# Three small edits to a transformer-block kernel: one query group moved ahead of a stage, three denominator sums put in one place, the last output block split in 384 and 128 columns

## The chip, the cores and the metric

The kernel runs on one core of one Trainium2 chip. The metric is the device time of one execution in microseconds (us). Beside it each run has a span, from the first to the last instruction in the trace of the core.

In the lines of the profile PE is TensorE (matmuls), PEld is TensorE's weight load (the stationary operand of a matmul), DVE is VectorE, ACT is ScalarE, POOL is GpSimd and SP is SyncE; a "q" behind it means the engine's sequencer, and "issue" is time in which an engine waited for nothing that the profile shows. L98 is the line of the helper `mm`, so the stages are told apart by the tiles. The "chain" is the sequence of work that ended last, followed back from the last instruction. To evacuate a PSUM tile is to read the result of its matmuls with another engine, which frees it. The landing of a DMA is the time from its issue to the moment its data is known to have arrived, and the closing waits are SyncE's waits for all DMAs at the end of the program.

## The reference, cut to what matters

One sequence of 2048 tokens, model width 1024, 32 attention heads of 32 columns, feed-forward width 3584, all in bf16. `sa, ca, ga, sb, cb, gb` are rows of 1024 computed from a conditioning vector.

```python
h = layernorm(x) * (1 + ca) + sa
q, k, v = split(h @ wqkv)                       # 32 heads
pq, pk = phi(q), phi(k)                         # phi(t) = (t + 1 if t > 0 else exp(t)) + 1e-6
kv  = einsum('bhsd,bhse->bhde', pk, v)          # linear attention: no softmax
z   = einsum('bhsd->bhd', pk)
num = einsum('bhqd,bhde->bhqe', pq, kv)
den = einsum('bhqd,bhd->bhq', pq, z) + 1e-6     # the denominator
x = x + ga * ((num / den) @ wo)
h = layernorm(x) * (1 + cb) + sb
x = x + gb * ((silu(h @ w_gate) * (h @ w_up)) @ w_down)
```

## The kernel before: the parts that matter

The sequence is cut into four chunks of 512 tokens (`sc`, 0 to 3). `pqs[sc]` holds phi(q), transposed: eight groups (`hg`) of 128 columns by 512 tokens. `SCW`, `NB` = 512; `STC` = 4 tiles of 128 tokens in a chunk; `FC` = 28 groups of the feed-forward width; `ST` = 16 tiles in all. The code below is cut and condensed.

The denominators of a chunk are sums on TensorE. Each matmul has 32 stationary columns and writes 32 rows of one PSUM tile, so four of them can run in the array together: in the trace of before the four start 3 to 4 ns apart, and each four take 0.056 us. The reciprocals travel through DRAM to be spread over the rows of their head (`rbc`), and `den_apply` multiplies them into `pq` in four VectorE operations of two head groups each.

```python
def den_norm(sc):
    pq = pqs[sc]
    den = acc_b("den")
    for hg in range(HG):
        for q in range(STC):
            mm(den[32*q:32*q+32, 0:P], lhsT=Zden[:, hg, :], rhs=pq[:, hg, q*P:(q+1)*P], ...)
    dsum = small.tile([P, P], F32, name="dsum", bufs=2)
    nc.vector.tensor_scalar_add(out=dsum[:], in0=den[:, 0:P], scalar1=DEN_EPS)
    rb = small.tile([P, P], BF16, name="rb", bufs=2)
    nc.vector.reciprocal(out=rb[:], in_=dsum[:])
    # ... rb to DRAM and back as rbc, by POOL's DMA queue (cut) ...

def den_apply(sc):
    pq, rbc = pqs[sc], rbcs.pop(sc)
    for k in range(4):
        ks = slice(2*k, 2*k+2)
        nc.vector.tensor_tensor(out=pq[:, ks, :], in0=pq[:, ks, :], in1=rbc[:, ks, :], op=ALU.mult)
```

A query group (`q_phase`) is eight 512-column matmuls followed by phi on ScalarE and VectorE. `wo_tile` multiplies 128 tokens of `pq` by `wo` in two blocks of eight matmuls. The order of work around the first wo stage and in the first gate and up stage is this:

```python
q_phase(2, 3, 4)
with tc.issue_after(last_phi[0].ins):
    den_apply(0)
q_phase(2, 4, 5)                  # one query group between the multiplies and wo
for st in range(STC):
    wo_tile(st)
q_phase(2, 5, 8)
q_phase(3, 0, 5)
# ... modulate, q_phase(3, 5, 8) (cut) ...
def late_den(apply, norm):
    if apply: den_apply(apply)
    if norm:  den_norm(norm)

# gate_up calls an entry after its block fb of 512 feed-forward columns
gate_up(0, {0: lambda: den_norm(1), 2: lambda: late_den(1, 2), 4: lambda: late_den(2, 3),
            6: lambda: den_apply(3)})
```

The last stage is `down`. Each output block of 128 tokens by 512 columns is 28 matmuls, two VectorE operations and one DMA out:

```python
for nb in range(NNB):
    ns = slice(nb*NB, (nb+1)*NB)
    x1r = x1p.tile([P, NB], F32, name="x1r", bufs=2)
    nc.sync.dma_start(out=x1r[:], in_=x1_dram[st*P:(st+1)*P, ns])
    y_ps = acc_a()
    for f in range(FC):
        mm(y_ps[:], lhsT=guT[sc][f//GPT][:, f%GPT, t*P:(t+1)*P], rhs=wd[f//WDF][:, f%WDF, ns], ...)
    yt = ep.tile([P, NB], F32, name="e")
    nc.vector.tensor_tensor(out=yt[:], in0=y_ps[:], in1=gb_bc[:, ns], op=ALU.mult)
    ob = yp.tile([P, NB], BF16, name="ob")
    nc.vector.tensor_tensor(out=ob[:], in0=yt[:], in1=x1r[:], op=ALU.add)
    nc.sync.dma_start(out=out2[st*P:(st+1)*P, ns], in_=ob[:])
```

Of the kernel before, what the change touches and what calls it, by code (L numbers as in the profile page):

```python
# [9 lines left out]
ALU = mybir.AluOpType  # L10
BF16 = mybir.dt.bfloat16
F32 = mybir.dt.float32
# [9 lines left out]
def kernel(  # L22
# [13 lines left out]
    nc = tc.nc  # L36
    P = nc.NUM_PARTITIONS
# [4 lines left out]
    ST = S // P  # L42
# [4 lines left out]
    NSC = S // SCW  # L47
    STC = SCW // P
    NB = 512
    NNB = D // NB  # L50
# [4 lines left out]
    GPT = 8  # L55
# [4 lines left out]
    out2 = out[0]  # L60
# [12 lines left out]
    x1p = ctx.enter_context(tc.tile_pool(name="x1p", bufs=3))  # L73
    ep = ctx.enter_context(tc.tile_pool(name="ep", bufs=3))
    yp = ctx.enter_context(tc.tile_pool(name="yp", bufs=2))
    small = ctx.enter_context(tc.tile_pool(name="small", bufs=4))
# [20 lines left out]
    def mm(out, lhsT, rhs, start, stop):  # L97
        return tc.keep_in_program_order(nc.tensor.matmul(out, lhsT=lhsT, rhs=rhs, start=start, stop=stop))  # L98
# [4 lines left out]
    def big(name, shape):  # L103
        return k8.tile([P] + shape, BF16, name=name, tag="k8")

    def acc_a():
        return pa.tile([P, NB], F32, name="acc", tag="pa")

    def acc_b(name, shape=(NB,), dt=F32):
        return pb.tile([P] + list(shape), dt, name=name, tag="pb")  # L110

    x1_dram = dram.tile([S, D], F32, name="x1_scratch")
# [16 lines left out]
    for b in range(2):  # L129
        ts = []  # L130
        for q in (1, 0):
            t = big("wme", [DC, NB])
# [36 lines left out]
    gb_bc = const.tile([P, D], BF16, name="gb_bc")  # L169
# [91 lines left out]
    def phi_to(dst, acc):  # L261
        e = ep.tile([P, NB], BF16, name="eb")
        nc.scalar.activation(out=e[:], in_=acc, func=ACT.Exp)  # L263
        nc.vector.tensor_scalar(out=e[:], in0=e[:], scalar1=1.0, scalar2=PHI_EPS, op0=ALU.min, op1=ALU.add)  # L264
        last_phi.append(None)
        last_phi[0] = last_phi[-1] = nc.vector.scalar_tensor_tensor(out=dst, in0=acc, scalar=0.0, in1=e[:], op0=ALU.max, op1=ALU.add)
# [36 lines left out]
    def q_phase(sc, lo=0, hi=DC):  # L303
        if lo == 0:
            pqs[sc] = big("pq", [HG, SCW])
        for qc in range(lo, hi):
            acc = acc_a()
            for cc in range(DC):
                mm(acc[:], lhsT=wq[cc // 4][:, cc % 4, qc * P:(qc + 1) * P], rhs=hTs[sc][:, cc, :],
                                 start=(cc == 0), stop=(cc == DC - 1))  # L310
            phi_to(pqs[sc][:, qc, :], acc[:])
# [55 lines left out]

    rbcs = {}

    def den_norm(sc):  # L370
        pq = pqs[sc]
        den = acc_b("den")
        for hg in range(HG):
            for q in range(STC):
                mm(den[32 * q:32 * q + 32, 0:P], lhsT=Zden[:, hg, :], rhs=pq[:, hg, q * P:(q + 1) * P],
                                 start=(hg == 0), stop=(hg == HG - 1))
        dsum = small.tile([P, P], F32, name="dsum", bufs=2)
        nc.vector.tensor_scalar_add(out=dsum[:], in0=den[:, 0:P], scalar1=DEN_EPS)
        rb = small.tile([P, P], BF16, name="rb", bufs=2)
        with nc.allow_low_precision("bf16 reciprocal multiplies bf16 phi(q)"):  # L380
            nc.vector.reciprocal(out=rb[:], in_=dsum[:])
        for q in range(STC):
            nc.gpsimd.dma_start(out=rden_dram[sc, :, q * P:(q + 1) * P], in_=rb[32 * q:32 * q + 32, :])
        rbc = big("rbc", [HG, SCW])
        rv = rden_dram[sc].rearrange("(h g) t -> h (g t)", h=HPC)
        for h in range(HPC):
            nc.gpsimd.dma_start(out=rbc[h * DH:(h + 1) * DH].rearrange("p g t -> p (g t)"),
                                in_=rv[h].unsqueeze(0).to_broadcast([DH, HG * SCW]))
        rbcs[sc] = rbc
# [4 lines that stand above are left out]
            ks = slice(2 * k, 2 * k + 2)  # L394
            nc.vector.tensor_tensor(out=pq[:, ks, :], in0=pq[:, ks, :], in1=rbc[:, ks, :], op=ALU.mult)  # L395
# [89 lines left out]
    for h in range(2):  # L485
        hs = slice(4 * h, 4 * h + 4)
        nc.vector.tensor_tensor(out=KVZ[:, hs, :], in0=kv_acc[:, hs, 0:P],
                                in1=kvmask[:].unsqueeze(1).to_broadcast([P, 4, P]), op=ALU.mult)
        nc.vector.tensor_tensor(out=Zden[:, hs, :], in0=kv_acc[:, hs, P:P + 1].to_broadcast([P, 4, DH]),
                                in1=zmask[:, hs, :], op=ALU.mult)  # L490
# [3 lines left out]
        transpose(tpk[:, hg, :], KVZ[:, hg, :])  # L494
    nc.scalar.copy(out=KVT[:, 0:4, :], in_=tpk[:, 0:4, :])
    nc.vector.tensor_copy(out=KVT[:, 4:8, :], in_=tpk[:, 4:8, :])
    den_norm(0)
    q_phase(1, 4, 5)
    wf = [(hg, nb) for hg in range(HG) for nb in range(NNB)]
    for qc in range(5, 11):  # L500
# [40 lines left out]
    guT = {}  # L541
# [3 lines left out]
    def gate_up(sc, between=None):  # L545
        guT[sc] = []
        for fb in range(NFB):
            wb = []
            for view in (wg_v, wu_v):
                w = big("wgu", [DC, FBW])  # L550
                last_w[sc] = nc.sync.dma_start(out=w[:], in_=view[:, :, fb * FBW:(fb + 1) * FBW])
                wb.append(w)
            for fj in range(FPB):
                f = fb * FPB + fj
                if f % GPT == 0:
                    guT[sc].append(big("gu", [min(GPT, FC - f), SCW]))
                ps = []
                for w in wb:
                    acc = acc_a()
                    for cc in range(DC):  # L560
                        last_mm[sc] = mm(acc[:], lhsT=w[:, cc, fj * P:(fj + 1) * P], rhs=h2Ts[sc][:, cc, :],
                                              start=(cc == 0), stop=(cc == DC - 1))
                    ps.append(acc)
                sg = ep.tile([P, NB], F32, name="e")
                nc.scalar.activation(out=sg[:], in_=ps[0][:], func=ACT.Silu)  # L565
                gm = nc.vector.tensor_tensor(out=guT[sc][f // GPT][:, f % GPT, :], in0=ps[1][:], in1=sg[:], op=ALU.mult)  # L566
            if between and fb in between:
                with tc.issue_after(gm.ins):
                    between[fb]()

    def down(sc, side):
        for t in range(STC):
            st = sc * STC + t
            for nb in range(NNB):
                ns = slice(nb * NB, (nb + 1) * NB)
                x1r = x1p.tile([P, NB], F32, name="x1r", bufs=2)
                nc.sync.dma_start(out=x1r[:], in_=x1_dram[st * P:(st + 1) * P, ns])
                y_ps = acc_a()
                for f in range(FC):
                    mm(y_ps[:], lhsT=guT[sc][f // GPT][:, f % GPT, t * P:(t + 1) * P],  # L580
                                     rhs=wd[f // WDF][:, f % WDF, ns], start=(f == 0), stop=(f == FC - 1))
                yt = ep.tile([P, NB], F32, name="e")
                nc.vector.tensor_tensor(out=yt[:], in0=y_ps[:], in1=gb_bc[:, ns], op=ALU.mult)  # L583
                ob = yp.tile([P, NB], BF16, name="ob")
                nc.vector.tensor_tensor(out=ob[:], in0=yt[:], in1=x1r[:], op=ALU.add)  # L585
                nc.sync.dma_start(out=out2[st * P:(st + 1) * P, ns], in_=ob[:])
                if side:
                    with tc.issue_after(last_mm[sc].ins):
                        side.pop(0)()

    q_phase(2, 3, 4)
    with tc.issue_after(last_phi[0].ins):
        den_apply(0)
    q_phase(2, 4, 5)
    for st in range(STC):
        wo_tile(st)
    q_phase(2, 5, 8)
    q_phase(3, 0, 5)
    with tc.issue_after(last_phi[0].ins):
        modulate_all(h2Ts[0], cb1T, sbT)  # L600
    q_phase(3, 5, 8)

    def late_den(apply, norm):
        if apply:
            den_apply(apply)
        if norm:
            den_norm(norm)

    gate_up(0, {0: lambda: den_norm(1), 2: lambda: late_den(1, 2), 4: lambda: late_den(2, 3),
                6: lambda: den_apply(3)})  # L610
    wd = []
    for b in range(FC // WDF):
        w = big("wd", [WDF, D])
# [2 lines left out]
    for sc in range(NSC):  # L616
        if sc > 0:
            gate_up(sc)
        side = []
        if sc + 1 < NSC:  # L620
            side = [lambda st=(sc + 1) * STC + t: wo_tile(st) for t in range(STC)]
        down(sc, side)
# [29 lines left out]
```

## Time and profile before

| | before |
|---|---|
| time, median of the runs beside the first run of the change | 847.84 us (847.76 to 847.96) |
| span of the profiled execution | 846.2 us |
| TensorE busy | 838.6 us, 99% |
| granted TensorE clock | 0.999 |

At 99% busy there seems to be nothing left to gain. But "busy" does not say that the engine moves at its best rate, and on a span of 846 us the missing 1% is 8 us. So one looks where the stream of matmuls is broken. In the stages without an interruption, 588 matmuls of 512 columns take 126.91 us in the chain, that is 0.2158 us each. Everything above that rate is loss.

**The first wo stage.** From the chain of waits of before (start us, length us, what):

```profile
180.57 1.74 PE acc L98 x8
...
182.96 0.31 DVE eb L264
...
183.29 0.04 DVE pq L266
...
183.90 0.69 DVE pq L395
184.59 0.05 issue
184.64 14.50 PE a_ps L98 x64
```

The chain leaves TensorE at 182.31 (the end of query group 3), goes over VectorE, and comes back at 184.64. The 64 wo matmuls then take 14.50 us where 64 x 0.2158 are 13.81. The timeline of the weight loads of before shows why (start, length, engine, line, operation; in brackets the idle time before it and what ended it):

```profile
183.43 0.10 PEld L98 LDWEIGHTS <-wq 128*128 128x128 bf16 x1
184.64 0.11 PEld L98 LDWEIGHTS <-pq 128*128 128x128 bf16 x2 [1.11 <-DVE pq L395]
185.24 0.11 PEld L98 LDWEIGHTS <-pq 128*128 128x128 bf16 x2 [0.49 <-DVE pq L395]
185.84 0.11 PEld L98 LDWEIGHTS <-pq 128*128 128x128 bf16 x2 [0.49 <-DVE pq L395]
186.44 0.55 PEld L98 LDWEIGHTS <-pq 128*128 128x128 bf16 x4 [0.49 <-DVE pq L395]
```

Two head groups are loaded, then TensorE waits for the next multiply of `den_apply(0)`, three times over. VectorE finishes one multiply every 0.60 us, and TensorE uses up two head groups in 0.43.

**The denominator sums.** From the timeline of TensorE in before, the first of the three blocks:

```profile
228.76 3.19 PE L98 MATMUL acc<-h2T,wgu 128*128 128x512 bf16 x14
231.87 0.63 PE L98 MATMUL den<-pq,Zden 128*32 128x128 bf16 x32
232.44 1.90 PE L98 MATMUL acc<-h2T,wgu 128*128 128x512 bf16 x8
```

The single records behind these lines: the last gate matmul starts at 231.565, the den matmuls at 231.874, and the next gate matmul at 232.437. Of those 0.872 us, 0.216 are the first matmul's own slot. So a block costs 0.656 us, and its eight head groups, 0.056 us apart, are only 0.45 of it.

The same trace has controls for reading the other 0.21 as the price of the 32-column mode. Where the matmuls go from 512 to 129 columns of `rhs`, with 128 stationary columns throughout (acc to kvp, at 64.999) and back (66.814), the next matmul starts one ordinary slot later, 0.216 and 0.056 us. Where 32 stationary columns begin or end, it does not: from acc to den it is 0.309 (0.093 more than the slot), from kvp to modr, the other matmuls with 32 stationary columns, 0.149 (0.093 more), and from modr back to acc 0.311 (0.095 more).

**The tail.** From the chain of before:

```profile
672.52 169.23 PE acc L98 x784
841.74 0.02 issue
841.77 0.70 DVE e L583
842.47 0.02 issue
842.49 0.69 DVE ob L585
```

After the last matmul come two VectorE operations on 512 columns, then the output DMA (issued at 843.214), its landing, and the closing waits, until 846.19. That is 4.46 us without any TensorE work.

### The profile page before, as it was taken

To read this page: it belongs to the slowest core of one execution; us is meant where nothing else is said; L and a number is where in the kernel's file an instruction comes from. 1 tells how busy PE (TensorE), PEld (TensorE's weight loads), DVE (VectorE), ACT (ScalarE), POOL (GpSimd) and SP (SyncE) were. 2 spreads that over 40 slices of the span, in tenths; PEclk is the share of its full clock that TensorE was granted. 3 is DMA by queue.
4 is the path that set the end of the run, shared out by engine and by line. 5 is a ranking of instruction groups with operands and counts; after the bars stand their busy time and mean duration, and the time that the engine had idled before them with its cause. 6 is when DMAs were issued, how large, how long until landed. Compare 5 with 4: busy or idle time off the path is not lost.

```text
span 846.2 us, 10498 instructions
## 1 busy us (share of the span) xinstructions
PE 838.6 (99%) x4284; PEld 385.7 (46%) x4284; DVE 307.2 (36%) x602; ACT 173.8 (21%) x267; POOL 55.7 (7%) x160
## 2 busy tenths in 40 slices
PE   8999999999999999999999999999999999999997
PEld 4445445544444444444444444444444444444443
DVE  5756464467423325431111344211114431111121
ACT  1455453354311110101111010011110101111000
POOL 2101010012011001100000010000001100000000
PEclk9999999999999999999999999999999999999999
DMA  9893870029976765528434073581604639710011
GB/s 309 301 257 98 243 187 1 1 52 215 348 210 207 214 186 174 181 69 266 146 104 149 19 236 95 159 283 54 199 1 126 185 69 318 240 59 0 19 57 50
DMA packets 125840, 128.74 MB, mean 152 GB/s; under 512 B 33376, under 2 KB 107360, under 8 KB 125280
## 3 DMA queue, kind: packets, MB, share of 16 engines
q1 hardware_dynamic: 122208, 115.36, 46.0%
q0 software_dynamic: 3584, 12.72, 5.0%
q8 instruction: 33, 0.54, 0.3%
q14 instruction: 15, 0.12, 0.0%
HBM read 108.01 MB, written 12.71 MB: 143 GB/s over the span
## 4 chain that ended last, share of the span: by engine, by line
PE 98%; DVE 1%; POOL 0%; DMA 0%; issue 0%; ACT 0%; SPq 0%; DVEq 0%; POOLq 0%
PE acc L98 88%; PE a_ps L98 7%; PE kvp L98 1%; PE modr L98 0%; PE wf L98 0%; DMA x_sb<-in_A_x_dram 0%; DVE stats L199 0%; PE mod_ps L98 0%; PE den L98 0%; POOL zmask L186 0%; PE tp L101 0%; POOL rstd L193 0%; PE bcr L98 0%; DVE e L583 0%; DVE ob L585 0%
## 5 line engine op out<-in xcount | busy, mean ns | idle before, releaser
L98 PE MATMUL acc<-h2T,wgu 128*128 128x512 bf16 x1792 | 387.9, 379 | 0.0
L98 PEld LDWEIGHTS <-wgu 128*128 128x128 bf16 x1792 | 175.1, 98 | 211.0
L98 PE MATMUL acc<-wd,gu 128*128 128x512 bf16 x896 | 196.0, 379 | 0.0
L566 DVE TENSOR_TENSOR gu<-acc,e 128x512 bf16<-128x512 f32 x112 | 77.4, 691 | 300.4 <-PE acc L98 300.4
L565 ACT ACTIVATE e<-acc 128x512 f32<-128x512 f32 x112 | 66.9, 597 | 375.2 <-PE acc L98 375.2
L98 PEld LDWEIGHTS <-gu 128*128 128x128 bf16 x896 | 87.6, 98 | 105.8
L98 PEld LDWEIGHTS <-hT 128*128 128x128 bf16 x512 | 49.6, 98 | 60.8 <-DVE hT L212 1.0
L583 DVE TENSOR_TENSOR e<-acc,gb_bc 128x512 f32<-128x512 f32 x32 | 22.1, 691 | 130.5 <-PE acc L98 130.5
L98 PE MATMUL a_ps<-wo,pq 128*128 128x512 bf16 x256 | 57.9, 379 | 0.6 <-DVE pq L395 0.6
L98 PE MATMUL acc<-hT,wq 128*128 128x512 bf16 x256 | 57.1, 379 | 0.0
L98 PE MATMUL acc<-wk,hT 128*128 128x512 bf16 x256 | 56.9, 379 | 0.0
L98 PE MATMUL acc<-wv,hT 128*128 128x512 bf16 x256 | 55.9, 379 | 0.0
L263 ACT ACTIVATE eb<-acc 128x512 bf16<-128x512 f32 x64 | 37.9, 596 | 62.8 <-PE acc L98 60.5
L209 ACT ACTIVATE xn<-x,nmr,rstd 128x1024 bf16<-128x1024 f32 x16 | 19.8, 1240 | 127.6 <-POOL nmr L207 127.6
L264 DVE TENSOR_SCALAR eb<-eb 128x512 bf16<-128x512 bf16 x64 | 18.4, 291 | 60.6 <-ACT eb L263 60.6
L98 PEld LDWEIGHTS <-pq 128*128 128x128 bf16 x256 | 24.7, 98 | 31.8 <-DVE pq L395 2.6
L98 PEld LDWEIGHTS <-wq 128*128 128x128 bf16 x256 | 24.9, 98 | 29.8
L534 POOL DMA_DIRECT2D x_scratch<-x x16 | 9.6, 600 | 369.6 <-DVE x L527 369.6
L527 DVE TENSOR_TENSOR x<-a_ps,x_sb 128x512 f32<-128x512 f32 x32 | 22.1, 691 | 8.0 <-PE a_ps L98 7.9
L193 POOL TENSOR_TENSOR rstd<-veps,neg_half 128x1 f32<-128x1 f32 x32 | 18.2, 569 | 81.3 <-DVE veps L191 70.4
L301 ACT CAST v<-acc 128x512 bf16<-128x512 f32 x32 | 18.3, 582 | 22.1 <-PE acc L98 22.1
L528 DVE BATCH_NORM_STATS2 stats<-x 128x6 f32<-128x512 f32 x32 | 22.2, 695 | 1.1
(72 smaller groups left out, 280.7 us busy)
## 6 DMA issues: line engine op xcount, KB each, us to landing
wgu<-in_B_w_gate_dram SPq DMA_DIRECT2D x28, 1024.0 KB, 7.4
wgu<-in_B_w_up_dram SPq DMA_DIRECT2D x28, 1024.0 KB, 8.7
x_sb<-in_A_x_dram SPq DMA_DIRECT2D x32, 256.0 KB, 5.9
wml<-in_w_mod_dram SPq DMA_DIRECT2D x8, 1024.0 KB, 8.6
x_scratch<-x POOLq DMA_DIRECT2D x16, 512.0 KB, 3.1
x1r<-x_scratch SPq DMA_DIRECT2D x32, 256.0 KB, 3.0
wd<-in_B_w_down_dram SPq DMA_DIRECT2D x7, 1024.0 KB, 7.7
wme<-in_w_mod_dram SPq DMA_DIRECT2D x4, 1024.0 KB, 11.2
```

The costliest lines, as they stand in the source:

```text
L98: return tc.keep_in_program_order(nc.tensor.matmul(out, lhsT=lhsT, rhs=rhs, start=start, stop=stop))
L193: nc.gpsimd.tensor_tensor(out=rstd[:, 0:n], in0=veps[:, 0:n], in1=neg_half[:].to_broadcast([P, n]), op=ALU.pow)
L209: nc.scalar.activation(out=dst, in_=src, func=ACT.Identity, bias=nmr[:], scale=rstd[:, 0:1])
L263: nc.scalar.activation(out=e[:], in_=acc, func=ACT.Exp)
L264: nc.vector.tensor_scalar(out=e[:], in0=e[:], scalar1=1.0, scalar2=PHI_EPS, op0=ALU.min, op1=ALU.add)
L301: nc.scalar.copy(out=v[:, t, nb * 4:(nb + 1) * 4, 0:P], in_=acc[:].rearrange("p (g e) -> p g e", e=P))
L527: nc.vector.tensor_tensor(out=x1[:, ns], in0=a_ps[:], in1=x_t[:, ns], op=ALU.add)
L528: nc.vector.bn_stats(out=stats[:, nb, :], in_=x1[:, ns])
L534: nc.gpsimd.dma_start(out=x1_dram[st * P:(st + 1) * P, :], in_=x1[:])
L565: nc.scalar.activation(out=sg[:], in_=ps[0][:], func=ACT.Silu)
L566: gm = nc.vector.tensor_tensor(out=guT[sc][f // GPT][:, f % GPT, :], in0=ps[1][:], in1=sg[:], op=ALU.mult)
L583: nc.vector.tensor_tensor(out=yt[:], in0=y_ps[:], in1=gb_bc[:, ns], op=ALU.mult)
```

## The change

Each edit aims at one of the three places. The diff, cut to its core:

```diff
-    def den_norm(sc):
+    def den_sum(sc):                     # matmuls, sum, reciprocal
...
+    def den_spread(sc):                  # rb to DRAM and back as rbc
...
+            pieces = [(0, NB), (NB, NB)] if st < ST - 1 else [(0, NB), (NB, 384), (NB + 384, 128)]
+            for lo, width in pieces:     # in down(): load, 28 matmuls, two VectorE operations, DMA out
...
     q_phase(2, 3, 4)
     with tc.issue_after(last_phi[0].ins):
         den_apply(0)
-    q_phase(2, 4, 5)
+    q_phase(2, 4, 6)
     for st in range(STC):
         wo_tile(st)
-    q_phase(2, 5, 8)
+    q_phase(2, 6, 8)
...
-    gate_up(0, {0: lambda: den_norm(1), 2: lambda: late_den(1, 2), 4: lambda: late_den(2, 3),
-                6: lambda: den_apply(3)})
+    def late_den(sc, sums=()):
+        for s in sums:
+            den_sum(s)
+        if sc > 1:
+            den_apply(sc - 1)
+        if sc < NSC:
+            den_spread(sc)
+
+    gate_up(0, {0: lambda: late_den(1, range(1, NSC)), 2: lambda: late_den(2), 4: lambda: late_den(3),
+                6: lambda: late_den(NSC)})
```

`den_norm(0)` becomes `den_sum(0)` and `den_spread(0)`; `dsum` goes to one buffer and `rb` to four.

More of the change, by code (lines that the diff above doesn't have):

```diff
@@ L368 @@
     rbcs = {}
-    def den_norm(sc):
+    rbs = {}
+    def den_sum(sc):
         pq = pqs[sc]
@@ L376, in den_norm @@
                                  start=(hg == 0), stop=(hg == HG - 1))
-        dsum = small.tile([P, P], F32, name="dsum", bufs=2)
+        dsum = small.tile([P, P], F32, name="dsum", bufs=1)
         nc.vector.tensor_scalar_add(out=dsum[:], in0=den[:, 0:P], scalar1=DEN_EPS)
-        rb = small.tile([P, P], BF16, name="rb", bufs=2)
+        rb = rbs[sc] = small.tile([P, P], BF16, name="rb", bufs=4)
         with nc.allow_low_precision("bf16 reciprocal multiplies bf16 phi(q)"):
             nc.vector.reciprocal(out=rb[:], in_=dsum[:])
+    def den_spread(sc):
+        rb = rbs.pop(sc)
         for q in range(STC):
@@ L496 @@
     nc.vector.tensor_copy(out=KVT[:, 4:8, :], in_=tpk[:, 4:8, :])
-    den_norm(0)
+    den_sum(0)
+    den_spread(0)
     q_phase(1, 4, 5)
@@ L573, in down @@
             st = sc * STC + t
-            for nb in range(NNB):
-                ns = slice(nb * NB, (nb + 1) * NB)
-                x1r = x1p.tile([P, NB], F32, name="x1r", bufs=2)
-                nc.sync.dma_start(out=x1r[:], in_=x1_dram[st * P:(st + 1) * P, ns])
-                y_ps = acc_a()
+            pieces = [(0, NB), (NB, NB)] if st < ST - 1 else [(0, NB), (NB, 384), (NB + 384, 128)]
+            for lo, width in pieces:
+                ns = slice(lo, lo + width)
+                x1r_t = x1p.tile([P, NB], F32, name="x1r", bufs=2)
+                x1r = x1r_t[:, 0:width]
+                nc.sync.dma_start(out=x1r, in_=x1_dram[st * P:(st + 1) * P, ns])
+                y_acc = acc_a()
+                y_ps = y_acc[:, 0:width]
                 for f in range(FC):
-                    mm(y_ps[:], lhsT=guT[sc][f // GPT][:, f % GPT, t * P:(t + 1) * P],
+                    mm(y_ps, lhsT=guT[sc][f // GPT][:, f % GPT, t * P:(t + 1) * P],
                                      rhs=wd[f // WDF][:, f % WDF, ns], start=(f == 0), stop=(f == FC - 1))
-                yt = ep.tile([P, NB], F32, name="e")
-                nc.vector.tensor_tensor(out=yt[:], in0=y_ps[:], in1=gb_bc[:, ns], op=ALU.mult)
-                ob = yp.tile([P, NB], BF16, name="ob")
-                nc.vector.tensor_tensor(out=ob[:], in0=yt[:], in1=x1r[:], op=ALU.add)
-                nc.sync.dma_start(out=out2[st * P:(st + 1) * P, ns], in_=ob[:])
+                yt_t = ep.tile([P, NB], F32, name="e")
+                yt = yt_t[:, 0:width]
+                nc.vector.tensor_tensor(out=yt, in0=y_ps, in1=gb_bc[:, ns], op=ALU.mult)
+                ob_t = yp.tile([P, NB], BF16, name="ob")
+                ob = ob_t[:, 0:width]
+                nc.vector.tensor_tensor(out=ob, in0=yt, in1=x1r, op=ALU.add)
+                nc.sync.dma_start(out=out2[st * P:(st + 1) * P, ns], in_=ob)
                 if side:
@@ L601 @@
     q_phase(3, 5, 8)
-    def late_den(apply, norm):
-        if apply:
-            den_apply(apply)
-        if norm:
-            den_norm(norm)
-    gate_up(0, {0: lambda: den_norm(1), 2: lambda: late_den(1, 2), 4: lambda: late_den(2, 3),
-                6: lambda: den_apply(3)})
+    def late_den(sc, sums=()):
[7 more added lines that the diff above has]
+                6: lambda: late_den(NSC)})
     wd = []
```

## The prediction

> **What bounds the kernel now.** The page gives TensorE 838.6 of 846.2 us busy (99%) at a granted clock of 0.999. The chain of waits that ended last is 98% PE. From about 16 us on, TensorE streams 512-column matmuls every 0.2158 us (126.91 us for 588 in the chain) and is broken in three places only, and each edit of the change is aimed at one.
>
> 1. *The first wo stage.* The timeline has the last query group (2, 4) at 182.1 to 183.9 us; the next weight load would be due at about 183.67. The first four loads of pq come at 184.64, 185.24, 185.84 and 186.44 instead: each waits for a 0.69 us multiply of den_apply(0), one every 0.60 us, while two matmuls use only 0.43. The load for head group 6 is due at 184.95 and comes at 186.44, so 1.49 us are lost. The 64 wo matmuls agree: 14.50 us instead of 13.81, after a late start of about 0.8.
> 2. *Denominator sums.* From the last 512-column matmul before a den block to the first after it are 0.872 us; 0.216 is that matmul's own slot, so a block costs 0.66. Its body is eight head groups at 0.056 us, or 0.45 (four 32-column tiles overlap). The other 0.21 are entering and leaving the 32-column mode. The Trainium skill ("TensorEngine Tiling (Array Packing)", Key Properties) says that changing the tiling mode drains TensorE; the gap on each side of the block here, about 0.1 us, agrees.
> 3. *The tail.* Matmuls end at 841.74; two VectorE operations on 128x512 (0.69 each) take until 843.21; the issue, landing (1.7 us) and final semaphore waits take until 846.2.
>
> **What the change does.**
> 1. One more query group (1.73 us) stands between den_apply(0) and wo. The built order keeps the four multiplies ahead of the phi operations of groups 4 and 5, so the multiplies still end at 184.6, 185.2, 185.8 and 186.4; loads are then due at 185.4, 185.8, 186.3 and 186.7. The wait goes, with 0.3 us to spare. Gain 1.47 us. The evacuation of wo starts about 1.3 us later on VectorE (188.5), but there are four PSUM tiles. h2T and the first gate weights come about 1 us later while gate_up starts 1.5 us sooner; their slack (about 3 us or more) should hold.
> 2. Three blocks become one: two exits and entries fewer, 2 x 0.21 = 0.41 us gained. VectorE gets 3 x 1.26 us of sums and reciprocals at once, under the 5 us until the gate/up evacuation needs it. No stall.
> 3. 28 extra matmuls. By the 129-column kvp matmuls (0.056 us apart), the last block grows by about 0.08 us. The last two VectorE operations shrink from 0.69 to about 0.29 us (dsum, 128 columns, takes 0.28): 0.80 gained. The 384 columns are evacuated during the last 28 matmuls. DMA latency is mostly fixed: the skill ("DMA: Bandwidth & Descriptors", two cost components) says about 2 us; 1.7 here, so nothing to gain. The last DMA's semaphore moves two places on in the closing waits (0.06 us each): 0.12. Net 0.84.
>
> Sum 2.7 us, all on the critical path: **845.1 us**, 8 in 10 within 844.7 to 845.8. Faster by over 2%: 0.00; within 2%: 1.00; slower: 0.00.
>
> **What would show it.** No VectorE wait before the first pq load; wo's 64 matmuls in 13.8 us; one den piece of about 1.45 us in the chain; last two VectorE operations near 0.29 us.
>
> **What would make it wrong.** Late h2T or wgu at the first gate matmul; VectorE's later wo evacuation filling the PSUM tiles; 128-column matmuls limited by weight loads (+0.7 us if 0.08 each); a slower landing of 256-byte rows.

## The result, and the profile after

The median is 845.63 us (four runs: 845.4, 845.63, 845.63, 847.27) against 847.84 us before. The ratio is 0.9974, with a 95% interval of 0.996 to 0.9989: a gain clear of the noise. The profiled span is 843.5 us against 846.2. The output was correct.

The first wo stage, from the chain of after: TensorE does not leave it any more, and the 64 matmuls take 13.81 us.

```profile
180.70 5.18 PE acc L98 x24
185.88 13.81 PE a_ps L98 x64
199.69 31.08 PE acc L98 x144
230.77 1.45 PE den L98 x96
232.22 89.03 PE acc L98 x412
```

The fourth line is the one den block that took the place of three. From the timeline of TensorE in after:

```profile
230.70 1.52 PE L98 MATMUL den<-pq,Zden 128*32 128x128 bf16 x96
```

The weight loads of after (timeline) have no wait in brackets:

```profile
183.34 2.04 PEld L98 LDWEIGHTS <-wq 128*128 128x128 bf16 x10
185.50 3.12 PEld L98 LDWEIGHTS <-pq 128*128 128x128 bf16 x15
```

The tail, from the chain of after. The two operations now take 0.30 and 0.29 us:

```profile
670.90 169.30 PE acc L98 x812
840.20 0.02 issue
840.23 0.30 DVE e L593
840.53 0.02 issue
840.55 0.29 DVE ob L596
```

And this is the timeline of VectorE in after, near the end: the 384 columns are evacuated while TensorE works on the last 128, and VectorE is then idle for 0.41 us before the last piece.

```profile
838.66 0.56 DVE L593 TENSOR_TENSOR e<-acc,gb_bc 128x384 f32<-128x384 f32 x1 [3.13 <-PE acc L98]
839.25 0.56 DVE L596 TENSOR_TENSOR ob<-e,x1r 128x384 bf16<-128x384 f32 x1
840.23 0.29 DVE L593 TENSOR_TENSOR e<-acc,gb_bc 128x128 f32<-128x128 f32 x1 [0.41 <-PE acc L98]
840.55 0.29 DVE L596 TENSOR_TENSOR ob<-e,x1r 128x128 bf16<-128x128 f32 x1
```

The landing of the last output DMA, in before and then in after (finer figures are given with the tail experiments):

```profile
DMA to landing us min/median/max: 1.7/1.7/1.7
DMA to landing us min/median/max: 1.5/1.5/1.5
```

All three mechanisms are visible as predicted. Two things are not as predicted. The span fell by 2.7 us and the time by only 2.2. And the time from the last output DMA's issue to the end fell by 0.35 us (2.98 to 2.63), where 0.12 had been forecast.

### The profile page after: what moved, and what is told of

It reads as the page before. It is cut to its first block, busy times and chain, and to the rows that moved or that the text cites. A ratio compares the mean times of both kernels' runs of the same rounds, so it can differ in the third digit from the quotient of the medians.

```text
span 843.5 us, 10565 instructions
## 1 busy us (share of the span) xinstructions
PE 838.6 (99%) x4312; PEld 388.2 (46%) x4312; DVE 307.8 (36%) x604; ACT 173.8 (21%) x267; POOL 55.7 (7%) x160
## 4 chain that ended last, share of the span: by engine, by line
PE 99%; DVE 0%; ACT 0%; issue 0%
PE acc L98 90%; PE a_ps L98 7%; PE kvp L98 1%; PE modr L98 0%; PE wf L98 0%; PE mod_ps L98 0%; PE tp L101 0%; PE den L98 0%; PE bcr L98 0%; ACT hT L220 0%; DVE hT L221 0%; PE mcol L98 0%; DVE e L593 0%; DVE ob L596 0%; DVE sel L402 0%
## 5 line engine op out<-in xcount | busy, mean ns | idle before, releaser
L98 PE MATMUL acc<-wd,gu 128*128 128x512 bf16 (+2 forms) x924 | 196.1, 373 | 0.0
L98 PEld LDWEIGHTS <-gu 128*128 128x128 bf16 x924 | 89.3, 98 | 104.5
L593 DVE TENSOR_TENSOR e<-acc,gb_bc 128x512 f32<-128x512 f32 (+2 forms) x33 | 22.3, 676 | 130.1 <-PE acc L98 130.1
L596 DVE TENSOR_TENSOR ob<-e,x1r 128x512 bf16<-128x512 f32 (+2 forms) x33 | 22.3, 675 | 1.0
```

The source lines that it names most:

```text
L98: return tc.keep_in_program_order(nc.tensor.matmul(out, lhsT=lhsT, rhs=rhs, start=start, stop=stop))
L593: nc.vector.tensor_tensor(out=yt, in0=y_ps, in1=gb_bc[:, ns], op=ALU.mult)
L596: nc.vector.tensor_tensor(out=ob, in0=yt, in1=x1r, op=ALU.add)
```

## The experiments

Twelve runs were made, on two chips (m_mid, t_onedma, t256 and t448 on one, the rest on the other). Each was timed against the kernel before in the same rounds. The first expectations speak of 1.6 us between time and span in before, and of 0.5 us of growth. That was 847.84, a median of four runs, less the one profiled span of 846.2; the later calls, with time and span of each run, have 1.84 to 1.89 in the median, and 0.3 us of growth. First the three parts alone, and the change once more.

### One part at a time

**g_only**: the kernel before with `q_phase(2, 4, 6)` and `q_phase(2, 6, 8)`, nothing else.

> The kernel before with one more query group ahead of the first wo stage, nothing else. Theory (three separate stalls that add up): the span falls by 1.3 us, the loss counted from the matmul starts of the two traces (the prediction had 1.47, counted from the weight loads); the 64 wo matmuls take 13.8 us without a wait for the multiplies. Rival (the stall only moves on): the later evacuation on VectorE comes back as a wait before the first gate matmul, and the span falls by under 0.6 us. On the 0.5 us by which time minus span grew from before to after: if it belongs to the last block, it does not show here and the time falls by about 1.3 too; if it differs from program to program or from load to load, it may show here.

Measured: 846.73 us against 848.09 (median of five and nine runs), span 844.85, which is 1.34 us less than before, ratio 0.9986 (0.9973 to 0.9998). No weight load waits for the multiplies, and the chain stays on TensorE from the query groups through wo. The rival, a stall that only moves on, falls. Time minus span is 1.89 us, and before it was also 1.89 in the same rounds.

**d_only**: the kernel before with `den_sum` and `den_spread` and the new hooks of the first gate and up stage.

> The kernel before with the sums of chunks 1 to 3 in one place, nothing else. Theory: the span falls by 0.42 us (two times the 0.21 of entering and leaving the 32-column mode); the den block is one piece of about 1.45 us. Rival (the saved 0.4 us of after is something else, a wait that moved): the span falls by under 0.15 us, or VectorE's six operations in a row make TensorE wait for an accumulator. Time minus span: as before (1.6 us) if the last block is its cause.

Measured: 847.56 us, span 845.73, 0.46 less than before. By the starts of the matmuls around it, the block of 96 costs 1.549 us, and the three of before cost 0.656, 0.657 and 0.657: a gain of 0.42. VectorE's six operations in a row delay nothing. The ratio of times is 0.9992 (0.9979 to 1.0004): by the times alone this gain does not stand clear of the noise, and it rests on the trace.

**t_only**: the kernel before with the last block in 384 and 128 columns.

> The kernel before with the last block in 384 and 128 columns, nothing else. Theory: the span falls by 1.1 us (0.80 by the two short VectorE operations, 0.23 by a faster landing, 0.12 by the place of the semaphore among the closing waits, less 0.07 for the extra matmuls). Rival for the last two: the landing differs from run to run, and the span falls by 0.8 us alone. Time minus span: if the 0.5 us belongs to the last block, the time falls by only 0.6 us and time minus span is 2.1 us, as in after; if not, the time falls by 1.1 us.

Measured: 847.15 us, span 845.21 in the profiled run and 845.0 in the median of the five. From the last matmul's end to the end of the span: 3.314 us, before 4.464, so 1.15 gained there, of which 0.07 goes to the extra matmuls. The last landing is 1.494 us, as in after (1.492), so it was not chance. The ratio of times is 0.9991 (0.9978 to 1.0003), so this part too is shown by the trace and not by the times. Time minus span is 2.15 us in the median: the excess of after is in this part. One of the five runs took 848.8 us with a span of 845.0 at full clock, 3.80 us apart, and why is not known.

**after_again**: the changed kernel, loaded again.

> The changed kernel unaltered, loaded again on the chip of the other three. If the 0.5 us outside the span belongs to the program, time minus span is again 2.1 us and the time about 845.6; if it belongs to one load of it, it may be 1.6 us and the time 845.1. The run at 847.27 us with a clock of 0.997 should not be the rule: at most one run of five like it.

Measured: 845.58 us, span 843.2, time minus span 2.20 (median). The excess belongs to the program, not to one load. The three parts' profiled spans fell by 1.34, 0.46 and 0.99, together 2.79; the whole change's by 2.69 in the first run and 2.99 in this one. The start of the kernel moves by some tenths from run to run, and none of the edits touches it; so count each span from its first kvp matmul instead. Then the three parts gain 1.31, 0.44 and 1.08, together 2.83, and the change gains 2.82 in both runs. The parts add up, as separate stalls on one chain should.

One of these five runs took 847.9 us, at a clock of 0.997. Such runs came in many of the kernels, before included (849.55), and a later profile caught one (t_samedma, below). The table of windows of after and of t_samedma for the stretch from 25 to 30 us (window; busy us and count of TensorE, weight loads, VectorE, ScalarE and GpSimd; then the granted clock, DMA share, GB/s):

```profile
25.00:30.00 5.00, 5.00 (x24) 2.12 (x23) 3.00 (x12) 0.28 (x1) 1.18 (x5) 1.00 1.05 387
```

```profile
25.00:30.00 5.00, 5.00 (x15) 1.92 (x16) 2.72 (x12) 0.00 (x0) 1.18 (x5) 0.66 1.05 384
```

With a clock of 0.66, 15 matmuls are done in the stretch instead of 24. The first kvp matmul of t_samedma starts at 66.54 us instead of 65.13. So that run lost its 1.5 us in the head, before any of the three places. That the other such runs, with clocks of 0.996 to 0.998, lost theirs in the same way is likely, but no trace of them shows it. None of their spans is used for a difference here, but the medians and ratios of times do contain them.

### The tail: size of the pieces, and where the time outside the span comes from

**m_mid**: the same split, but in a block where it shortens nothing.

```diff
-            pieces = [(0, NB), (NB, NB)] if st < ST - 1 else [(0, NB), (NB, 384), (NB + 384, 128)]
+            pieces = [(0, NB), (NB, NB)] if st != ST - 2 else [(0, NB), (NB, 384), (NB + 384, 128)]
```

> The kernel before with the 384 and 128 columns in the second tile from the end, where they shorten nothing: same 28 extra matmuls, same two extra DMAs as the change, the last block whole. The span should be that of before plus 0.07 us (846.1 to 846.3). It tells apart where the 0.3 us outside the span comes from that t_only and after show (time minus span 2.15 us, before 1.87): if from the larger program or the larger number of DMAs, it is 2.15 here too; if from how the last output leaves, it stays 1.87.

Measured: 848.38 us against 847.99, span 846.1, time minus span 2.14 us. The 0.3 us have nothing to do with how the last output leaves: they come with the split here too. The medians are 0.4 us apart, but the interval of the ratio (0.9987 to 1.0015) does not set the times apart; time minus span does (2.11 to 2.41 against 1.81 to 1.91 in before).

One part of the gain in the tail is here all the same. From the seen landing to the end of the span it is 1.14 us, as in after, and not 1.26: two more DMAs anywhere put the last one's wait two places further on among the closing waits (one more, in t_onedma below, gives 1.20; none more, in t_samedma, 1.26).

**t_onedma**: the change, with both pieces in one output tile and one DMA out.

```diff
+                if lo % NB == 0:
+                    ob_t = yp.tile([P, NB], BF16, name="ob")
...
+                if o + width == NB:
+                    nc.sync.dma_start(out=out2[st*P:(st+1)*P, lo-o:lo+width], in_=ob_t[:])
```

> The changed kernel, but both pieces of every block are written to one output tile that leaves by one DMA of 1024-byte rows after the second piece. The last VectorE operations stay at 0.29 us. Theory (the landing goes by the row size): landing again 1.72 us instead of 1.49, one closing wait more, span up by 0.3 us to about 843.5; if the time outside the span belongs to the short rows of the last DMA it falls back to 1.87 us and the time stays at about 845.4. Rival (the landing is chance): landing about 1.5, span about 843.3. Second rival: time minus span stays 2.15, and the time is 845.7.

Measured: 845.82 us, span 843.67. The last DMA, again 128 KB, lands 1.765 us after its issue, and time minus span is 2.15: the second rival. So the fast landing was not chance: with the whole block in one DMA it is slow again, and the second output DMA is worth its place, since three quarters of the block are already on their way. All these DMAs have 128 rows, so bytes and row size change together, and which of the two counts is not told apart.

**t256**: pieces of 256 and 256 columns.

> The changed kernel with the last block in 256 and 256 columns. The last two VectorE operations take 0.42 us each (0.158 fixed and 1.04 ns per column) instead of 0.29, the last matmul 0.05 more: span up by 0.3 us to about 843.5. Landing with 512-byte rows between 1.49 and 1.72 if it goes by row size. Time minus span: 2.15 if any second DMA at the end causes it, less if the row size does.

Measured: 845.88 us, span 843.72, landing 1.593 us, time minus span 2.18. The two last VectorE operations took 0.425 and 0.426 us.

**t448**: pieces of 448 and 64 columns.

> The changed kernel with the last block in 448 and 64 columns. The last two VectorE operations take 0.22 us each, but the 28 last matmuls (0.03 us apart, 0.82 us) are too short to hide the two operations on 448 columns (0.62 each), so the last pair starts about 0.5 us late: span up by about 0.3 us to 843.5, although the last piece is the smallest. Rival (the smaller the last piece, the better): span down by 0.13 us. Landing with 128-byte rows 1.4 us or less if it goes by row size; time minus span 2.15 or more.

Measured: 846.02 us (two of the five runs had a clock of 0.997; the lowest is 845.74), span 843.63. VectorE's timeline near the end:

```profile
839.24 0.62 DVE L593 TENSOR_TENSOR e<-acc,gb_bc 128x448 f32<-128x448 f32 x1 [3.88 <-PE acc L98]
839.90 0.62 DVE L596 TENSOR_TENSOR ob<-e,x1r 128x448 bf16<-128x448 f32 x1
840.44 0.22 DVE L593 TENSOR_TENSOR e<-acc,gb_bc 128x64 f32<-128x64 f32 x1
840.69 0.23 DVE L596 TENSOR_TENSOR ob<-e,x1r 128x64 bf16<-128x64 f32 x1
```

The last pair starts at 840.44 although TensorE was done at 840.02, and no wait for TensorE stands before it: VectorE itself was late, with the 448 columns. The rival, "the smaller the last piece, the better", falls. Its span, 843.63, is above that of 384 and 128 (843.2 to 843.5), and so is that of two halves (843.72). These two ran on another chip than after_again, and starts differ; but from the last matmul's end to the end of the span, which depends on neither start, it is 3.32 us in after, 3.68 in t256 and 3.61 in t448.

The last DMA's landing, from its issue to the moment the closing wait for it ends, by the bytes of its 128 rows: 1024-byte rows 1.718 us (before), 1.733 (m_mid), 1.765 (t_onedma); 512-byte rows 1.593; 256-byte rows 1.492 (after). t448's 128-byte rows were at most 1.55, but that DMA was issued only 0.4 us after the one of the 448 columns and shares the queue with it; that this is the reason is not shown.

**t_samedma**: as t_onedma, and the pieces also share one load of x1, so the DMA count is that of before.

> The changed kernel with the pieces of a block sharing one load of x1 and one output DMA, so it has as many DMAs as before and still 28 matmuls more. It tells apart what makes time minus span 2.15 instead of 1.87: if the two extra DMAs, it is 1.87 here; if the 56 extra TensorE instructions, 2.15. Span as t_onedma, 843.7 (landing 1.75 us with 1024-byte rows).

Measured: 845.86 us, time minus span 2.06 (1.94 to 2.34). The profiled execution is one with the low clock in the head, so its span (845.3) is not compared; the three runs at a clock of 0.999 and above had 843.5 to 843.8.

**m_dmaonly**: the kernel before with two more DMAs and whole matmuls.

```diff
+                cuts = [(0, NB)] if (st, nb) != (ST - 2, NNB - 1) else [(0, 384), (384, NB)]
+                for lo, hi in cuts:      # the load of x1r; the same loop around the DMA out
+                    nc.sync.dma_start(out=x1r[:, lo:hi], ...)
```

> The kernel before, with only the load of x1 and the output DMA of the block two from the end split into 384 and 128 columns: two more DMAs, not one more TensorE instruction. The counterpart of t_samedma: time minus span 2.15 if DMAs make it, 1.87 if TensorE instructions do. Span 846.1 to 846.2.

Measured: 848.05 us against 848.13, span 846.2, time minus span 1.90. The landing-to-end part falls to 1.14 us here as in m_mid. Two DMAs more do not bring the excess of time over span; taking them away (t_samedma) does not remove most of it.

### One group more still, and one operation less

**g2**: the change with `q_phase(2, 4, 7)` and `q_phase(2, 7, 8)`.

> The changed kernel with two more query groups ahead of the first wo stage instead of one. Theory (the wait for the four multiplies was 1.3 us and one group of 1.73 covers it): nothing more to gain, span as after (843.2 to 843.5), no wait for pq. VectorE takes up wo about 1.0 us later still. Rival (more work ahead always helps, another wait of PE is left there): the span falls by 0.2 us or more. Second rival (VectorE's later evacuation fills the accumulators): the span rises.

Measured: span 843.4 in the profile (843.4 twice, 843.7, and two runs with clocks of 0.998 and 0.996), time 846.13 in the median and 845.52 at best, with no wait for pq and none before the gate matmuls. A second group brings nothing: the wait was used up by the first.

**fold**: the change with the last 128 columns of `gb` multiplied into w_down beforehand.

```diff
+    FOLD = D - 128
+    def fold(b):                         # called after block b of the last gate_up
+        nc.vector.tensor_tensor(out=wd[b][:, :, FOLD:D], in0=wd[b][:, :, FOLD:D],
+                                in1=gb_bc[:, FOLD:D].unsqueeze(1).to_broadcast([P, WDF, D - FOLD]), op=ALU.mult)
+        if b == FC // WDF - 1:
+            nc.vector.memset(gb_bc[:, FOLD:D], 1.0)
...
-                nc.vector.tensor_tensor(out=yt, in0=y_ps, in1=gb_bc[:, ns], op=ALU.mult)
+                if lo < FOLD: ...        # as before
+                else: yt = y_ps
```

> The changed kernel, with the gate of the last 128 output columns multiplied into those columns of w_down during the last gate and up stage (seven VectorE operations of 0.5 to 0.7 us, where VectorE is idle four fifths of the time), and 1.0 written into the gate row there. The last piece then needs one VectorE operation between its last matmul and the output DMA instead of two. If the tail is a plain chain as the two traces say, the span falls by 0.33 us against after (to about 843.0) and the time to about 845.2; rival: the extra operations delay an evacuation in gate_up and TensorE waits, or the output is off by the extra rounding.

Measured: 844.80 us in the median of six (844.56 to 846.87; two of them at a clock of 0.998) against 848.13, ratio 0.9964 (0.9951 to 0.9978), output correct. It has the lowest median of all kernels run, and the ratio of the change in its two calls was 0.9974 and 0.9976, but the intervals overlap and the two did not run in the same rounds. The seven extra operations take 0.41 us each, and no matmul of gate_up waits. The last stretch of VectorE's timeline:

```profile
839.90 0.29 DVE L607 TENSOR_TENSOR ob<-acc,x1r 128x128 bf16<-128x128 f32 x1 [0.41 <-PE acc L98]
```

From the last matmul's end to the end of the span it is 3.16 us against 3.31 to 3.32 in after, so the tail gained 0.15 of the 0.33 expected. The last DMA is now issued 0.70 us after the one of the 384 columns (after: 1.03), and its landing, counted as above, is 1.67 us instead of 1.49. The rest of the lower time is outside the span: time minus span is 1.78 us here.

### Time minus span, all kernels

| kernel | matmuls more than before | DMAs more than before | time minus span, median, us |
|---|---|---|---|
| before | 0 | 0 | 1.89, 1.85, 1.84 |
| g_only, d_only | 0 | 0 | 1.89, 1.86 |
| m_dmaonly | 0 | 2 | 1.90 |
| t_samedma | 28 | 0 | 2.06 |
| t_onedma | 28 | 1 | 2.15 |
| m_mid, t_only, t256, t448 | 28 | 2 | 2.14, 2.15, 2.18, 2.14 |
| after (two calls), g2 | 28 | 2 | 2.15, 2.20, 2.18 |
| fold | 28 | 2 | 1.78 |

The single runs lie between 1.80 and 1.92 in before, g_only and d_only, between 2.09 and 2.43 in the kernels with the split, t_samedma (1.94 to 2.34) and fold (1.76 to 1.95) aside, and two runs are far out (2.87 in after_again, 3.80 in t_only). The spans of single runs are on record to 0.1 us only. Except for the last row, the excess goes with the split, not with the DMAs and not with the place of the split. The split brings 28 extra matmuls with their weight loads, and also two more VectorE operations; no run tells these apart. fold has 28 more matmuls too, and still more VectorE operations, and does not show it. So "a larger TensorE program costs 0.3 us outside the span" is not the cause, or not all of it. What this time consists of, no trace here shows, since it lies outside the recorded instructions. It stays open.

## Why the prediction was right

The time on record was 845.1 us, within 844.7 to 845.8. Measured: 845.63 and 845.58. The direction, the three places and the absence of a new stall were right; three terms of the sum were mis-sized, in both directions, and partly cancelled. That was luck: without the unforeseen 0.23 us of the faster landing, the time would have been about 845.86 (an estimate from 845.63), outside the range.

The prediction's "three places only" is not quite so. In before and after alike TensorE also waits 0.4 us for `hT` at about 23 us, and the price of the 32-column mode is still paid around den of chunk 0 and around two modr blocks.

1. **First wo stage: 1.47 us forecast, 1.31 to 1.34 measured.** The prediction measured how late the weight load for head group 6 came (1.49 us). In the running stream here a load starts 0.21 us ahead of its matmul (185.499 and 185.713 in after). A load that is released late has its matmul right behind it (both at 184.64). So lateness by loads counts 0.16 us that the matmuls did not lose. By the chain: from 180.57 to 199.14 are 18.57 us for 80 matmuls, 17.26 at the undisturbed rate, so 1.31 were lost; in after, 18.99 us for 88 are exactly the rate. g_only gave 1.34 by the span, and 1.31 counted from its first kvp matmul.
2. **Denominator sums: 0.41 us forecast, 0.42 measured** in d_only and after (three blocks of 0.656, 0.657 and 0.657, one of 1.549). What a second and third block saves is entering and leaving. That switching the tiling mode drains TensorE is what the Trainium skill says ("TensorEngine Tiling (Array Packing)", Key Properties); the runs show the price, about 0.1 us on each side, at den and at modr and not at borders without such a change, and do not show the inside of it.
3. **Tail: 0.84 us forecast, 1.08 measured in the span.** VectorE: 0.80 forecast; from its start to the DMA issue 1.447 us before and 0.646 after, so 0.80. Extra matmuls: 0.08 forecast, 0.07 measured. Closing waits: 0.12 forecast; from the seen landing to the end of the span 1.262 us before and 1.141 after, so 0.12; m_mid and m_dmaonly have it too. **The step that failed is "so nothing to gain" about the landing**: it fell from 1.72 to 1.49 us, by 0.23. The prediction named the Trainium skill's two cost components ("DMA: Bandwidth & Descriptors", Anatomy of one DMA) and used only the fixed one. The page also gives the variable one, bytes over 436e9 per second, in a fit for DMAs issued from GpSimd, while these are issued from SP: an estimate from it for 128 KB and 32 KB is 0.30 and 0.08 us, a difference of 0.23 before rounding. The measured 0.23 agrees, and t256's 1.593 us for 64 KB lies between. But t448 (16 KB, at most 1.55 us) and fold (32 KB, 1.67), whose last DMA follows another by 0.4 and 0.7 us, do not fit, so the size alone does not settle a landing.
4. **What the sum left out.** The time was computed from the span with a constant distance. That distance is 1.84 to 1.89 us before and 2.15 to 2.20 after, so 0.3 us of the gain were given back outside the span. Which part carries it is shown (the split, in every kernel that has it but fold); why is open. In the second call that closes the account: 2.82 less 0.3 is 2.52, and the time fell by 2.51. In the first the time fell by 2.21 only, since before ran at 847.84 there and at 847.99 to 848.13 in the later calls; the spans of those first runs are not on record, and this other 0.3 stays open. The head of the profiled execution of after also started its steady stream 0.13 us later, by chance of that run.

Together, in the two profiles: 1.31 + 0.42 + 1.08 less 0.13 in the head makes 2.68 of the 2.69 us by which the spans differ.

The warnings were checked too. VectorE's later start on wo (188.03 instead of 187.23 us) filled no PSUM tile, h2T and the gate weights were in time, and the 128-column matmuls ran 0.056 us apart. The rows of 256 bytes landed faster, not slower.

## What to carry to other kernels

On an engine that is 99% busy, take the rate of its undisturbed stream and count every stretch against it; three gaps were found that way, each could be cut alone, by 0.4 to 1.3 us, and the gains added up. Count the loss at the starts of the matmuls, not at the weight loads. When the last block is split to shorten the tail, the last piece should be small, so that what follows it is short (halves lost by longer last operations, 0.43 us instead of 0.29, and a slower landing), but the piece before it must be evacuated while the last one computes (448 and 64 lost there). And compare the time as well as the span, since an edit can change what lies outside the trace.

## What the Trainium skill lacked or had wrong

- "TensorE: Matmul & The Clock Gate", Back-to-back issue gap: for a stream of weight-load and matmul pairs it gives about 131 ns at 512 columns and 81 ns at 128, and calls N/2.4 + 2.5 ns the gap of an isolated matmul (further up the same page gives 215.7 ns at 512 and 55.6 at 128 as measured for back-to-back matmuls). In these traces the sustained stream of such pairs runs at 215.8 ns with 512 columns, 162.5 ns with 384 and 55.8 ns with 128: the formula (215.8, 162.5, 55.8) and the passage further up fit the stream, and the 131 and 81 do not.
- "DMA: Bandwidth & Descriptors", Anatomy of one DMA (two cost components): the fixed part is given as about 2.0 us, in a fit for DMAs issued from GpSimd. For SBUF-to-HBM DMAs issued from SP, the whole landing was 1.72 us for 128 KB, 1.59 for 64 KB and 1.49 for 32 KB, so about 1.4 us fixed, an estimate by taking off the page's variable part, which agrees for these three. Where another DMA had been issued 0.4 or 0.7 us before, the landing was longer than that (at most 1.55 for 16 KB, 1.67 for 32 KB).
- "TensorEngine Tiling (Array Packing)", Key Properties: it says that a mode switch drains TensorE, without a number. Entering and leaving the 32-column mode cost 0.21 us a block here (0.656 less 0.448 for the body).
- No page was found that has the time between the span and the measured time, 1.78 to 2.20 us in the median here, depending on the program. "Runtime: NRT & Kernel Launch" has other intervals around a kernel and does not relate them to such a span.
